# Computing the convolution of the first 1024 tokens with diagonal matmuls instead of a banded matrix and a DRAM bounce

## The chip, the cores and the metric

The kernel runs on one core of one Trainium2 chip. The metric is device time in microseconds (us) of the whole program, the median of several executions. Executions of the same kernel differ by some tenths of a per cent, here by up to 4.8 us (the kernel before, 768.03 to 772.8).

## The reference

The program is a causal convolution with 7 taps over the sequence, followed by a two-layer network with an ELU between the layers. There are 8 heads of 24 channels, and all channels of a head share 7 softmax-normalised taps.

```python
w = softmax(weight, axis=-1)                      # (8 heads, 7 taps)
x_pad = concat([zeros(B, 6, D), x], axis=1)       # x: (8, 4096, 192)
x_unf = x_pad[:, idx, :].reshape(B, S, 7, 8, 24)
att = einsum('hk,bskhg->bshg', w, x_unf).reshape(B * S, 192)
h = att @ w_in                                    # 192 -> 2048
g = where(h > 0, h, exp(minimum(h, 0)) - 1)
out = g @ w_out                                   # 2048 -> 192
```

## The kernel before

The 32,768 tokens are cut into 32 "supers" of 1024 tokens. A super has 16 "pairs" (blocks of 128 of the 2048 hidden columns, for two half supers at once). For each pair TensorE computes H = att @ w_in into one of three PSUM slots, ScalarE computes E = exp(H), GpSimd clips E to at most 1, and VectorE writes gT = max(E - 1, H), which frees the slot. While super s+1 makes its H, TensorE multiplies the gT of super s by w_out ("output matmuls").

The convolution is also done on TensorE: x times a banded matrix `Tm` that holds the 7 taps on its diagonals. The band is built through DRAM: zeros are written, then the taps along the diagonal, and the result is read back into `Tk`. The order of `Tk` is not that of `Tm`, so one engine copies it. The convolved data is evicted to `csb`, bounced through DRAM (`conv_slots`) and gathered into `att`, the layout that the H matmuls need.

```python
# sync engine: the band through DRAM
sy.dma_start(band[...], Tm[...]).then_inc(s_band, 16)             # zeros
W(s_set, 5)                                                       # softmaxed taps are ready
sy.dma_start(diagonal, wprb[...]).then_inc(s_band, 16)            # 128 pieces of 112 bytes
W(s_band, 32)
sy.dma_start(Tk[:], band[:, :, :]).then_inc(s_band, 16)
# ... cut ...
# VectorE, before its loop (super 0 reads Tk itself; Tm is for the later supers)
v.tensor_copy(Tm[:, :, :].rearrange("p h t -> p t h"), Tk[:]).then_inc(s_tm)
# ... cut ...
# ScalarE, each pair n
W(s_h, n + 1)
for u in range(2):
    a.activation(E[:, n % NE, u, :], H[:, k, GS * u : GS * (u + 1)], ACT.Exp).then_inc(s_exp)
```

The convs of the next super are placed at fixed pairs (`EARLY_CONV = {1: (1, 0), 4: (1, 1), 12: (2, 0)}` during super 0).

## Time and profile before

| | before |
|---|---|
| median of the first three runs | 769.51 us (768.03 to 772.8) |
| span of the profiled execution | 767.1 us |
| first H of super 0 starts | 27.41 us |
| first exp starts | 28.27 us |
| first H of super 1 starts | 52.13 us |

The table of busy time by stretches, for 50 to 750 us. The columns are the window and its length, then busy us and instruction count of TensorE, its weight loads, VectorE, ScalarE and GpSimd, then granted clock, DMA share and GB/s.

```profile
50.00:750.00 700.00, 699.84 (x13274) 489.44 (x13270) 610.31 (x992) 620.30 (x1113) 631.59 (x1058) 1.00 0.43 95
```

TensorE is busy for 699.84 of 700 us at full clock. Nothing can be gained there without removing matmuls. What is open is the head.

The head's part of the chain of waits before: start, duration (both us), and what the program was waiting for or doing.

```profile
0.75 2.96 DMA wq<-in_weight_dram
...
5.49 5.64 DMA conv_band<-wprb
...
11.15 4.94 DMA Tk<-conv_band
...
16.13 3.89 PE H L466 x76
...
20.04 1.24 DVE csb L402
...
21.29 2.17 DMA conv_slots<-csb
...
24.88 2.40 DMA att<-conv_slots
...
41.52 9.73 DMA w_out<-in_moe_w_out_dram
```

Seven things follow one another before the first H can start at 27.41: loading the taps, storing the diagonal, reading the band back, the conv, its eviction, the bounce and the gather. The change attacks this chain. Later the chain runs through the w_out load, for which the first output matmul, at 51.30, waited 0.16 us.

### The profile page before, as it was taken

Reading aid. Unit: us, or ns where it says so; the run is one execution under the profiler, and the core shown is the slowest. Engines: PE = TensorE matmul, PEld = TensorE weight load, DVE = VectorE, ACT = ScalarE, POOL = GpSimd, SP = SyncE. Lnnn points to the kernel's source line nnn. Section 1 sums busy time; section 2 is a strip of 40 time slices with the busy share of each in tenths; the row PEclk is TensorE's granted clock in tenths of the full one; section 3 lists DMA queues with packets and bytes.
Section 4 is the critical chain, followed back from the end, with each engine's and each line's share of the span. In section 5 each row is a group of like instructions: output and inputs, shape, how many; then the busy total and the mean of one; then the engine's idle time right before and its main releaser. Section 6 shows DMA issues by size and latency. Waiting matters only on the chain.

```text
span 767.1 us, 32323 instructions
## 1 busy us (share of the span) xinstructions
PE 752.3 (98%) x13910; PEld 515.0 (67%) x13910; DVE 638.7 (83%) x1035; ACT 645.2 (84%) x1155; POOL 661.8 (86%) x1109
## 2 busy tenths in 40 slices
PE   6899999999999999999999999999999999999997
PEld 3347767666766776776776677677676667767766
DVE  1588898898898898889888889888888988988993
ACT  1488888888888988888888888898888898888883
POOL 3498998899898899899889989989989988988892
PEclk8999999999999999999999999999999999999999
DMA  7474344345435435534434543543553443454211
GB/s 119 103 126 107 78 104 96 92 100 114 85 90 113 86 87 114 110 78 101 107 81 100 115 88 87 115 86 89 111 110 78 102 104 83 100 114 91 71 44 63
DMA packets 107919, 73.73 MB, mean 96 GB/s; under 512 B 45408, under 2 KB 106848, under 8 KB 107776
## 3 DMA queue, kind: packets, MB, share of 16 engines
q1 hardware_dynamic: 66344, 55.14, 23.7%
q0 software_dynamic: 40944, 16.13, 19.3%
q8 instruction: 109, 1.79, 1.0%
q10 hardware_dynamic: 488, 0.39, 0.2%
q14 instruction: 34, 0.28, 0.1%
HBM read 44.34 MB, written 42.24 MB: 113 GB/s over the span
## 4 chain that ended last, share of the span: by engine, by line
PE 93%; DMA 4%; DVE 1%; POOL 1%; ACT 0%; issue 0%; SPq 0%; POOLq 0%
PE ops L521 44%; PE H L492 44%; PE H L466 5%; DMA w_out<-in_moe_w_out_dram 1%; DMA conv_band<-wprb 1%; PE H L521 1%; DVE gT L413 1%; DMA Tk<-conv_band 1%; POOL E L310 0%; DMA wq<-in_weight_dram 0%; DMA att<-conv_slots 0%; ACT E L367 0%; DMA conv_slots<-csb 0%; POOL w_in L280 0%; PE ops L445 0%
## 5 line engine op out<-in xcount | busy, mean ns | idle before, releaser
L413 DVE SCALAR_TENSOR_TENSOR gT<-E,H 128x512 f16<-128x512 f32 x1024 | 630.6, 682 | 100.3 <-POOL E L310 92.8
L310 POOL TENSOR_SCALAR E<-E 128x512 f32<-128x512 f32 x1024 | 603.7, 612 | 71.0 <-ACT E L367 67.2
L367 ACT ACTIVATE E<-H 128x512 f32<-128x512 f32 x1024 | 546.1, 605 | 92.8 <-PE H L492 79.2
L521 PEld LDWEIGHTS ops<-w_out,gT 64*128 64x128 f16 x8064 | 342.3, 94 | 109.9 <-ACT osb L341 10.9
L521 PE MATMUL ops<-w_out,gT 64*128 64x192 f16 x8064 | 414.5, 243 | 1.1 <-DVE gT L413 0.9
L492 PE MATMUL H<-att,w_in 64*128 64x512 bf16 x3072 | 407.3, 378 | 3.5 <-DMA att<-conv_slots 2.0
L492 PEld LDWEIGHTS H<-att,w_in 64*128 64x128 bf16 x3072 | 129.8, 94 | 105.5 <-DVE gT L413 5.9
L356 ACT ACTIVATE csb<-H 128x1024 bf16<-128x1024 f32 x63 | 64.5, 1023 | 13.7 <-PE H L466 13.7
L341 ACT ACTIVATE osb<-ops 128x768 f32<-128x768 f32 x63 | 51.6, 818 | 5.1 <-PE ops L521 5.1
L275 POOL DMA_DIRECT2D xg<-in_x_dram x64 | 53.8, 842 | 0.4 <-issue 0.4
L466 PE MATMUL H<-Tm,xg 128*24 128x122 bf16 (+1 forms) x2480 | 40.7, 209 | 0.6 <-DVE gT L413 0.6
L466 PEld LDWEIGHTS H<-Tm,xg 128*24 128x24 bf16 x2480 | 31.3, 92 | 11.2 <-issue 11.2
L445 PE MATMUL ops<-zw 128*128 128x512 bf16 x86 | 24.2, 421 | 1.2 <-DVE zw L378 1.2
L445 PEld LDWEIGHTS ops<-zw 128*128 128x128 bf16 x86 | 7.8, 106 | 15.0 <-issue 8.9
L280 POOL DMA_DIRECT2D w_in<-in_moe_w_in_dram x6 | 3.5, 611 | 15.7 <-DMA att<-conv_slots 15.7
L402 DVE CAST csb<-H 128x1024 bf16<-128x1024 f32 x1 | 1.2, 1225 | 12.4 <-PE H L466 12.4
L466 PE MATMUL H<-Tk,xg 128*24 128x122 bf16 (+1 forms) x80 | 3.9, 363 | 4.7 <-DMA Tk<-conv_band 4.7
L424 DVE COPY osb<-H 128x384 f32<-128x384 f32 x1 | 0.6, 558 | 8.9 <-PE H L521 8.9
L466 PEld LDWEIGHTS H<-Tk,xg 128*24 128x24 bf16 x80 | 2.3, 117 | 6.4 <-DMA Tk<-conv_band 5.2
L521 PE MATMUL H<-w_out,gT 64*128 64x192 f16 x128 | 5.6, 243 | 0.1
L521 PEld LDWEIGHTS H<-w_out,gT 64*128 64x128 f16 x128 | 5.2, 94 | 0.3 <-PE H L521 0.3
L333 ACT ACTIVATE osb<-H 128x384 f32<-128x384 f32 x1 | 0.5, 490 | 4.7 <-PE H L521 4.7
(21 smaller groups left out, 13.3 us busy)
## 6 DMA issues: line engine op xcount, KB each, us to landing
out_dram<-osb SPq DMA_DIRECT2D x127, 192.0 KB, 2.7
conv_slots<-csb SPq DMA_DIRECT2D x64, 256.0 KB, 2.5
att<-conv_slots SPq DMA_DIRECT2D x189, 64.0 KB
xg<-in_x_dram POOLq DMA_DIRECT2D x31, 240.0 KB, 5.1
xg<-in_x_dram POOLq DMA_DIRECT2D x33, 192.0 KB, 4.5
w_in<-in_moe_w_in_dram POOLq DMA_DIRECT2D x6, 128.0 KB, 5.1
w_out<-in_moe_w_out_dram POOLq DMA_DIRECT2D x1, 768.0 KB, 9.7
w_in<-w_in POOLq DMA_DIRECT2D x1, 384.0 KB, 5.1
```

Source lines behind the costliest of these rows:

```text
L275: g.dma_start(xg[:, b, w0:w1, :], src).then_inc(s_x[b][part - 1], 16)
L280: g.dma_start(w_in[0:HP, j, c0:c1], bass.AP(tensor=moe_w_in.tensor, offset=8 * j * FF + c0, ap=[[CPH * FF, HEADS], [FF, 8], [1, c1 - c0]], ...
L310: g.tensor_scalar(out=E[:, n % NE, u, :], in0=E[:, n % NE, u, :], scalar1=1.0, scalar2=0.0, op0=ALU.min, op1=ALU.max,).then_inc(s_clp)
L341: a.activation(osb[:, b, :, :, :].rearrange("p g k d -> p g (k d)"), ops[:, :, 0 : 2 * D], ACT.Copy,).then_inc(s_oev)
L356: a.activation(csb[:, m % 4, :, :], H[:, slot_of_conv[m] % 3, :].rearrange("p (b t) -> p b t", b=2), ACT.Copy,).then_inc(s_ce)
L367: a.activation(E[:, n % NE, u, :], H[:, k, GS * u : GS * (u + 1)], ACT.Exp).then_inc(s_exp)
L402: v.tensor_copy(csb[:, 1, :, :], H[:, slot_of_conv[1] % 3, :].rearrange("p (b t) -> p b t", b=2),).then_inc(s_cd)
L413: v.scalar_tensor_tensor(out=gT[:, s % NG3, q, u, :], in0=E[:, n % NE, u, :], scalar=1.0, in1=H[:, slot_of_pair[n] % 3, GS * u : GS * (u + ...
L445: pe.matmul(ops[:, 0, :], zw[:, 0:P], zw[:], start=True, stop=True)
L466: ins = pe.matmul(H[SLOT * q : SLOT * q + CPH, k % 3, GS * hb + o : GS * hb + o + nc_], xg[:, s % NXB, w, CPH * h : CPH * (h + 1)], Tm[:, ...
L492: ins = pe.matmul(H[:, k % 3, GS * r : GS * (r + 1)], w_in[HP * r : HP * (r + 1), j, FC * q : FC * (q + 1)], att[HP * r : HP * (r + 1), s ...
L521: ins = pe.matmul(acc[:, g, D * kb : D * (kb + 1)], gT[HP * rt : HP * (rt + 1), t % NG3, q, g, t0 : t0 + P], w_out[HP * rt : HP * (rt + 1) ...
```

## The change: its intent and its diff

The first super no longer uses the band or the bounce. x is loaded in plain rows and turned by TensorE with an identity matrix. Then eight matmuls with diagonal weights (`Dg`), accumulated in PSUM, do the 7 taps for two neighbouring tokens. The channel order becomes 3p+j, so w_in can be loaded straight into both halves of the partitions, without an on-chip copy. The band is still built, because the supers from 1 on use it. The diff, cut to what matters here:

```diff
-QA = 8
-WARM = (34, 24, 2)
+WCOLS = ((0, 512), (512, 1280), (1280, 2048))
+WARM = (12, 2)
-EARLY_CONV = {1: (1, 0), 4: (1, 1), 12: (2, 0)}
+EARLY_CONV = {5: (1, 0), 8: (1, 1), 13: (2, 0)}
@@ TensorE, before its loop
+            for i in range(3):
+                for j in range(3):
+                    turn(xt_bank(j)[:, P * i : P * (i + 1)], 3 + 2 * i, j, 0, P)
 ... cut ...
+                for k in range(KSIZE + 1):
+                    for r in range(2):
+                        ins = pe.matmul(head_bank(j, r), Dg[HP*r : HP*(r+1), k : k+2, :],
+                            xT[HP*r : HP*(r+1), j, k : k+GS-1 : 2], start=(k == 0), stop=(k == KSIZE), ...)
@@ VectorE, before its loop
+            W(s_tp, 3)
+            v.tensor_copy(xT[:, 1, PAD : PAD + GS], xt_bank(1)).then_inc(s_xtd)
             W(s_wex, 1)
             v.tensor_reduce(wsum[:], wex[:], AXIS.X, ALU.add).then_inc(s_set)   # taps of the band
 ... cut ...
-            v.tensor_copy(Tm[:, :, :].rearrange("p h t -> p t h"), Tk[:]).then_inc(s_tm)
@@ ScalarE, before its loop (so before its first exp)
+            W(s_hc, 3)
+            a.activation(*head_out(a, 2, 0, 1), ACT.Copy).then_inc(s_ha)
+            W(s_band, 48)
+            a.activation(
+                Tm[:, :, :].rearrange("p h t -> p t h"), Tk[:], ACT.Copy
+            ).then_inc(s_tm)
@@ GpSimd, before its loop
+            load_head(0)      # x of super 0; then an identity by select, load_head(1), load_head(2)
+            load_w_in(0)
+            load_w_in(1)
+            for part in (1, 2):
                 load_x(1, part)
-            W(s_w[0], 48)  ... w_in[HP:P] <- w_in[0:HP], W(s_att[0], ...), load_w_in(1)
+            load_w_in(2)
```

The output rows of super 0 are written in the new token order. Everything from super 1 on is the same work.

More of the change, by code (lines that the diff above doesn't have):

```diff
@@ L30 @@
 LAG = -1
-QA = 8
-WARM = (34, 24, 2)
+WCOLS = ((0, 512), (512, 1280), (1280, 2048))
+Q_PART = (0,) * 4 + (1,) * 6 + (2,) * 6
+WARM = (12, 2)
 HALF_STEPS = (10, 10, 6, 6, 10, 11, 11)
 CONV_AT = ((4, 1, 1), (12, 2, 0))
-EARLY_CONV = {1: (1, 0), 4: (1, 1), 12: (2, 0)}
+EARLY_CONV = {5: (1, 0), 8: (1, 1), 13: (2, 0)}
 XW = 5
@@ L89, in conv_at @@
     def conv_at(s, g):
-        m = 2 * s + g
+        m = 2 * s + g - 2
         slot_of_conv[m] = take_slot(("c", m))
         order.append(("c", m))
-    for g in range(2):
-        conv_at(0, g)
     rounds_at = {}
@@ L141, in sema @@
             return stack.enter_context(nc.semaphore(name))
+        xh = sbuf("xh", [P, 9, D], BF16)
+        ident = sbuf("ident", [P, P], BF16)
+        mask = sbuf("mask", [P, HP], BF16)
+        Dg = sbuf("Dg", [P, 9, HP], BF16)
+        xT = sbuf("xT", [P, 3, GS + 8], BF16)
+        wd = sbuf("wd", [P, KSIZE], FP32)
+        wdm = sbuf("wdm", [P, 1], FP32)
+        wd2 = sbuf("wd2", [P, KSIZE], FP32)
+        wde = sbuf("wde", [P, KSIZE], FP32)
+        wds = sbuf("wds", [P, 1], FP32)
+        wdr = sbuf("wdr", [P, 1], FP32)
         xg = sbuf("xg", [P, NXB, NWIN, D], BF16)
@@ L165, in bass_lightweight_conv__then__act_elu_kernel @@
         s_wq = sema("s_wq")
-        s_w = [sema(f"s_w{i}") for i in range(3)]
+        s_w = [sema(f"s_w{i}") for i in range(4)]
+        s_wd = sema("s_wd")
+        s_xl = [sema(f"s_xl{i}") for i in range(3)]
+        s_id = sema("s_id")
+        s_one = sema("s_one")
+        s_z0 = sema("s_z0")
+        s_v = sema("s_v")
+        s_de = sema("s_de")
+        s_D = sema("s_D")
+        s_tp = sema("s_tp")
+        s_xta = sema("s_xta")
+        s_xtd = sema("s_xtd")
+        s_hc = sema("s_hc")
+        s_ha = sema("s_ha")
+        s_hd = sema("s_hd")
         s_set = sema("s_set")
@@ L169, in bass_lightweight_conv__then__act_elu_kernel @@
         s_scr = sema("s_scr")
-        s_hz = sema("s_hz")
         s_x = [[sema(f"s_x{i}_{g}") for g in range(2)] for i in range(NXB)]
         s_tm = sema("s_tm")
-        s_cd = sema("s_cd")
         s_od = sema("s_od")
-        s_wdp = sema("s_wdp")
         s_z = sema("s_z")
@@ L184, in bass_lightweight_conv__then__act_elu_kernel @@
         s_dw = [sema(f"s_dw{i}") for i in range(4)]
-        s_wd = [sema(f"s_wd{i}") for i in range(2)]
         s_tz = sema("s_tz")
@@ L204, in __call__, with xt_bank, head_bank @@
                     self.eng.wait_ge(sem, value)
-        WCOLS = ((0, P * QA), (P * QA, FF))
         NDMA_ATT = 6
-        x_need, z_need, x_count, z_count = {}, {}, [0] * NXB, 0
-        for s in range(NS):
-            x_count[s % NXB] += 16 + 16 * (s == 0)
-            z_count += s % SPB == 0
-            x_need[s, 0] = x_count[s % NXB]
-            x_need[s, 1] = 16 * (s // NXB + 1)
-            z_need[s] = z_count
+        x_need, z_need = {}, {}
+        for s in range(1, NS):
+            x_need[s, 0] = x_need[s, 1] = 16 * ((s - 1) // NXB + 1)
+            z_need[s] = s // SPB
+        def xt_bank(j):
+            return H[:, j // 2, GS * (j % 2) : GS * (j % 2 + 1)]
+        def head_bank(j, r):
+            if j == 0:
+                return ops[:, r, 0 : GS // 2]
+            return H[:, (0, 2, 0)[j], GS * r : GS * r + GS // 2]
         def conv_read(W, m):
-            if m == 1:
-                W(s_cd, 1)
-            else:
-                W(s_ce, m + (m == 0))
+            W(s_ce, m + 1)
         def out_group(eng, t, half, g):
@@ L225, in out_group @@
             row = SUP * t + GS * g + 2 * P * half
-            eng.dma_start(
-                out[row : row + 2 * P, :].rearrange("(k p) d -> p k d", p=P),
-                osb[:, b, g, :, :],
-            ).then_inc(s_out[b], 16)
+            dst = out[row : row + 2 * P, :].rearrange("(k p) d -> p k d", p=P)
+            if t == 0:
+                dst = bass.AP(
+                    tensor=out.tensor,
+                    offset=(GS * half + 1 - g) * D,
+                    ap=[[2 * D, P], [2 * P * D, 2], [1, D]],
+                )
+            eng.dma_start(dst, osb[:, b, g, :, :]).then_inc(s_out[b], 16)
         def read_att(eng, W, s, g):
-            m = 2 * s + g
+            m = 2 * s + g - 2
             W(s_dw[m % 4], 16 * (m // 4 + 1))
@@ L237, in read_att @@
                     tensor=bounce.tensor,
-                    offset=(2 * P * (s % 2) + 8 * j) * SUP + GS * g,
-                    ap=[[SLOT * SUP, HEADS], [SUP, 8], [1, GS]],
+                    offset=(2 * P * (s % 2) + j) * SUP + GS * g,
+                    ap=[[SLOT * SUP, HEADS], [3 * SUP, 8], [1, GS]],
                 )
@@ L254, in load_x @@
                 if part == 0:
-                    if s:
-                        W(s_x[b][0], x_need[s, 0])
+                    W(s_x[b][0], x_need[s, 0])
                     g.memset(xg[0:PAD, b, 0, :], 0.0).then_inc(s_z)
-                    if s == 0:
-                        g.dma_start(
-                            xg[PAD:P, b, 0, :], x_flat[0 : P - PAD, :]
-                        ).then_inc(s_x[b][0], 16)
                     return
-                if s >= NXB:
-                    W(s_cv, 2 * (s - NXB) + 2)
+                if s > NXB:
+                    W(s_cv, 2 * (s - NXB))
                 if part == 1:
-                    w0, w1, row = int(s == 0), XW, t0 - PAD + CW * (s == 0)
+                    w0, w1, row = 0, XW, t0 - PAD
                 else:
@@ L278, in load_w_in, with load_head @@
                 c0, c1 = WCOLS[k]
-                for j in range(3):
+                for r in range(2):
                     g.dma_start(
-                        w_in[0:HP, j, c0:c1],
-                        bass.AP(
-                            tensor=moe_w_in.tensor,
-                            offset=8 * j * FF + c0,
-                            ap=[[CPH * FF, HEADS], [FF, 8], [1, c1 - c0]],
-                        ),
-                    ).then_inc(s_w[k], 16)
-            for part in range(3):
-                load_x(0, part)
+                        w_in[HP * r : HP * (r + 1), :, c0:c1],
+                        moe_w_in.rearrange("(p j) f -> p j f", j=3)[:, :, c0:c1],
+                    ).then_inc(s_w[k], 16)
+            def load_head(k):
+                slot, tile, count = ((3, 0, 3), (4, 4, 3), (1, 3, 2))[k]
+                g.dma_start(
+                    xh[:, slot : slot + 2 * count - 1 : 2, :] if k < 2 else xh[:, 1:3, :],
+                    bass.AP(
+                        tensor=x_flat.tensor,
+                        offset=tile * P * D,
+                        ap=[[D, P], [(1 if k < 2 else 4) * P * D, count], [1, D]],
+                    ),
+                ).then_inc(s_xl[k], 16)
+            load_head(0)
+            W(s_one, 1)
+            g.affine_select(
+                out=ident[:],
+                in_=ident[:],
+                pattern=[[-1, P]],
+                compare_op=ALU.is_equal,
+                fill=0.0,
+                base=0,
+                channel_multiplier=1,
+            ).then_inc(s_id)
+            load_head(1)
+            load_head(2)
             load_w_in(0)
-            for part in range(3):
+            load_w_in(1)
+            for part in (1, 2):
                 load_x(1, part)
-            W(s_w[0], 48)
-            c0, c1 = WCOLS[0]
-            g.dma_start(w_in[HP:P, :, c0:c1], w_in[0:HP, :, c0:c1]).then_inc(s_wdp, 16)
-            W(s_att[0], 16 * NDMA_ATT)
-            load_w_in(1)
+            load_w_in(2)
             for n in range(NP):
@@ L303, in _gpsimd @@
                         w_out[:, :, :], moe_w_out.rearrange("(q p) d -> p q d", p=FC)
-                    ).then_inc(s_w[2], 16)
+                    ).then_inc(s_w[3], 16)
                 for at, part in X_AT:
@@ L324, in _scalar, with head_out @@
             a.activation(scr[:, 1:2], scr[:, 0:1], ACT.Exp)
+            W(s_v, 3)
+            a.activation(wde[:], wd2[:], ACT.Exp, accum_out=wds[:]).then_inc(s_de)
             W(s_set, 2)
             a.activation(wex[:], wq2[:], ACT.Exp).then_inc(s_wex)
+            W(s_tp, 1)
+            a.activation(
+                xT[:, :, 0:PAD],
+                H[:, 1, GS : GS + 24].rearrange("p (j c) -> p j c", j=3)[:, :, 0:PAD],
+                ACT.Copy,
+            ).then_inc(s_xta)
+            for j in (0, 2):
+                W(s_tp, j + 2)
+                a.activation(xT[:, j, PAD : PAD + GS], xt_bank(j), ACT.Copy).then_inc(s_xta)
+            def head_out(eng, j, r0, r1):
+                src = ops if j == 0 else H[:, (0, 2, 0)[j], :].rearrange("p (r t) -> p r t", r=2)
+                return (
+                    att[:, 0, j, GS // 2 * r0 : GS // 2 * r1].rearrange("p (r t) -> p r t", r=r1 - r0),
+                    src[:, r0:r1, 0 : GS // 2],
+                )
+            W(s_hc, 1)
+            a.activation(*head_out(a, 0, 0, 2), ACT.Copy).then_inc(s_ha)
+            W(s_hc, 3)
+            a.activation(*head_out(a, 2, 0, 1), ACT.Copy).then_inc(s_ha)
+            W(s_band, 48)
+            a.activation(
+                Tm[:, :, :].rearrange("p h t -> p t h"), Tk[:], ACT.Copy
+            ).then_inc(s_tm)
             def evac(t, half):
@@ L349, in _scalar @@
                     m = item[1]
-                    if m == 1:
-                        W(s_dw[0], 16)
-                        read_att(a, W, 0, 0)
-                        continue
                     W(s_cv, m + 1)
@@ L379, in _vector @@
             v.memset(Tm[:], 0.0).then_inc(s_tz)
+            v.memset(ident[:], 1.0).then_inc(s_one)
+            v.memset(xh[:, 0, :], 0.0).then_inc(s_z0)
+            v.memset(Dg[:, ::8, :], 0.0).then_inc(s_z0)
+            W(s_id, 1)
+            v.tensor_tensor(mask[:], ident[:, 0:HP], ident[:, HP:P], ALU.add).then_inc(s_v)
+            W(s_wd, 32)
+            v.tensor_reduce(wdm[:], wd[:], AXIS.X, ALU.max).then_inc(s_v)
+            W(s_v, 2)
+            v.tensor_scalar(
+                out=wd2[:], in0=wd[:], scalar1=wdm[:, 0:1], scalar2=None, op0=ALU.subtract
+            ).then_inc(s_v)
             W(s_wq, 16)
@@ L388, in _vector @@
             ).then_inc(s_set)
+            W(s_de, 1)
+            v.reciprocal(wdr[:], wds[:]).then_inc(s_v)
+            W(s_v, 4)
+            v.scalar_tensor_tensor(
+                out=Dg[:, 1:8, :],
+                in0=mask[:, :].unsqueeze(1).to_broadcast([P, KSIZE, HP]),
+                scalar=wdr[:, 0:1],
+                in1=wde[:, :].unsqueeze(2).to_broadcast([P, KSIZE, HP]),
+                op0=ALU.mult,
+                op1=ALU.mult,
+            ).then_inc(s_D)
+            W(s_tp, 3)
+            v.tensor_copy(xT[:, 1, PAD : PAD + GS], xt_bank(1)).then_inc(s_xtd)
             W(s_wex, 1)
@@ L399, in _vector @@
             ).then_inc(s_set)
-            v.memset(H[:, 0:2, :], 0.0).then_inc(s_hz)
-            W(s_cv, 2)
+            W(s_hc, 2)
             v.tensor_copy(
-                csb[:, 1, :, :],
-                H[:, slot_of_conv[1] % 3, :].rearrange("p (b t) -> p b t", b=2),
-            ).then_inc(s_cd)
-            v.tensor_copy(Tm[:, :, :].rearrange("p h t -> p t h"), Tk[:]).then_inc(s_tm)
+                att[:, 0, 1, :].rearrange("p (r t) -> p r t", r=2),
+                H[:, 2, :].rearrange("p (r t) -> p r t", r=2)[:, :, 0 : GS // 2],
+            ).then_inc(s_hd)
+            W(s_hc, 3)
+            v.tensor_copy(
+                att[:, 0, 2, GS // 2 : GS], H[:, 0, GS : GS + GS // 2]
+            ).then_inc(s_hd)
             for n in range(NP):
@@ L445, in warm, with turn @@
                     pe.matmul(ops[:, 0, :], zw[:, 0:P], zw[:], start=True, stop=True)
-            warm(WARM[0])
+            def turn(dst, slot, j, c0, c1):
+                return pe.matmul(
+                    dst,
+                    xh[:, slot : slot + 2, :].rearrange("p i d -> p (i d)")[:, j::3],
+                    ident[:, c0:c1],
+                    start=True,
+                    stop=True,
+                )
+            warm(WARM[0])
+            W(s_id, 1)
+            W(s_xl[0], 16)
+            W(s_xl[1], 16)
+            for i in range(3):
+                for j in range(3):
+                    turn(xt_bank(j)[:, P * i : P * (i + 1)], 3 + 2 * i, j, 0, P)
+            W(s_xl[2], 16)
+            W(s_z0, 1)
+            for j in range(3):
+                ins = turn(H[:, 1, GS + 8 * j : GS + 8 * j + PAD], 0, j, P - PAD, P)
+            ins.then_inc(s_tp)
+            for j in range(3):
+                turn(xt_bank(j)[:, 3 * P : GS], 1, j, 0, P).then_inc(s_tp)
+            W(s_D, 1)
+            W(s_z0, 2)
+            for j in range(3):
+                W(s_xta, (2, 2, 3)[j])
+                if j:
+                    W(s_xtd, 1)
+                for k in range(KSIZE + 1):
+                    for r in range(2):
+                        ins = pe.matmul(
+                            head_bank(j, r),
+                            Dg[HP * r : HP * (r + 1), k : k + 2, :],
+                            xT[HP * r : HP * (r + 1), j, k : k + GS - 1 : 2],
+                            start=(k == 0),
+                            stop=(k == KSIZE),
+                            tile_position=(HP * r, 0),
+                        )
+                ins.then_inc(s_hc)
             for item in order:
@@ L450, in _tensor @@
                     m = item[1]
-                    s, g = divmod(m, 2)
+                    s, g = divmod(m + 2, 2)
                     if m == 0:
-                        W(s_band, 48)
-                        W(s_hz, 1)
-                    if m == 2:
                         W(s_tm, 1)
@@ L469, in _tensor @@
                                     xg[:, s % NXB, w, CPH * h : CPH * (h + 1)],
-                                    Tm[:, h, PAD + c0 : PAD + c0 + nc_]
-                                    if s
-                                    else Tk[:, PAD + c0 : PAD + c0 + nc_, h],
+                                    Tm[:, h, PAD + c0 : PAD + c0 + nc_],
                                     start=True,
@@ L481, in _tensor @@
                     if n == 0:
+                        W(s_ha, 2)
+                        W(s_hd, 2)
+                    elif n < NQ - 1:
                         warm(WARM[1])
-                    elif n < NQ - 1:
-                        warm(WARM[2])
-                    W(s_w[q // QA], 48)
-                    W(s_wdp if q < QA else s_wd[1], 16)
-                    W(s_att[s % 2], 16 * NDMA_ATT * (s // 2 + 1))
+                    W(s_w[Q_PART[q]], 32)
+                    W(s_att[s % 2], 16 * NDMA_ATT * ((s + 1) // 2))
                     k = slot_of_pair[n]
@@ L502, in _tensor @@
                     _, t, half, r0, r1 = item
-                    W(s_w[2], 16)
+                    W(s_w[3], 16)
                     if (t, half) == last_half:
@@ L536, in _sync @@
             W = Waits(sy)
+            for r in range(2):
+                sy.dma_start(
+                    wd[HP * r : HP * (r + 1), :],
+                    bass.AP(
+                        tensor=weight.tensor, offset=0, ap=[[KSIZE, HEADS], [0, 8], [1, KSIZE]]
+                    ),
+                ).then_inc(s_wd, 16)
             sy.dma_start(
@@ L555, in _sync @@
             sy.dma_start(Tk[:], band[:, :, :]).then_inc(s_band, 16)
-            def copy_w(k):
-                W(s_w[k], 48)
-                c0, c1 = WCOLS[k]
-                sy.dma_start(w_in[HP:P, :, c0:c1], w_in[0:HP, :, c0:c1]).then_inc(s_wd[k], 16)
             for item in order:
@@ L564, in _sync @@
                     m = item[1]
-                    s, g = divmod(m, 2)
+                    s, g = divmod(m + 2, 2)
                     conv_read(W, m)
@@ L570, in _sync @@
                     ).then_inc(s_dw[m % 4], 16)
-                    if m == 1:
-                        read_att(sy, W, 0, 1)
-                        copy_w(1)
-                    elif m == 2 or g == 1:
+                    if m == 0 or g == 1:
                         read_att(sy, W, s, g)
```

## The prediction

> **What bounds it now.** TensorE. The table by stretches gives it 699.8 busy us out of 700 between 50 and 750 us, granted clock 1.00; the change touches nothing there (the 3p+j order only re-addresses equal-sized transfers). Only the head is open: the first exp starts at 28.3 us and the output matmuls start at 51.3 us (timeline).
>
> **The head before.** The chain of waits is serial: weight load 3.0 us, softmax 1.7, band diagonal store 5.6, band read-back 4.9, conv matmuls 3.9, eviction 1.2, bounce write 2.2, gather 2.4-4, so H begins at 27.4. From there, 15 pairs take about 23 us, paced by GpSimd and VectorE (1.3 us per pair, plus about 1 us per conv taking a PSUM slot).
>
> **What the change does to the first super.** x lands at about 7.5-8.5 us (the old loads took 3.5-7.1 us), turns under 1 us, one 128x512 copy about 0.6, 48 taps of 256 columns, about 2.6 us warm or 5.2 cold (the trace has a 512-column pair at 0.22 warm), half-bank copies 0.7. So H would start at about 13-15 us: about 13 us earlier.
>
> **Why most of that will not be cashed.** ScalarE's program now waits for the read-back band and copies it into Tm *before its first exp*. VectorE computes the band weights only *after* its copy of xT. So the band chain starts later than before: wprb at about 9.9 us instead of 5.4; diagonal store about 5.6 (it was 5.6 for 14 KB, with the DMA engines saturated); read-back about 5; hence Tk at about 20.5-21. W_in is now fetched twice, so the DMA load is no lighter. [...] the 14 KB store took 5.6 us under load, an earlier 28 KB load 3.0. Then the Tm copy, 1.2-2.6 us (VectorE took 2.58 for it). First exp at about 22-23.5 us: 5-6 us earlier, not 13.
>
> **The first 15 pairs after.** Again about 23 us; the convs move to pairs 5, 8 and 13, about 0.5 us better since none disturbs the fill. Against it, TensorE fills three slots by about 16 us and idles about 8 us, so it resumes at half clock ([...]before, the granted clock was 0.50 from 14 to 20 us after an idle from 11.4). With two warming matmuls per pair that costs about 1 us. Output matmuls start at about 46.5 us instead of 51.3; after that nothing changes.
>
> **Sum.** 28.3 to 22.9 is -5.4, the cold clock +1.0, the better conv order -0.5: about -5 us. Predicted 764.5 us, 8 in 10 between 760.0 and 768.0. Chances: faster by over 2% 0.02, within 2% 0.975, slower 0.005. Even 13 us would be under 2%.
>
> **Right or wrong in the profile.**
> - First H before 16 us, but first exp after 21, with ScalarE's Tm copy directly before it, waiting for the DMA Tk.
> - Diagonal store issued at about 10 us; the head's chain runs through wprb, store, read-back, Tm, exp.
> - Granted clock 0.5 around 20-26 us.
> - Output matmuls from about 46.5; afterwards supers of 22.65 us as before.
>
> **What would make it wrong.** Store and read-back at 2-3 us each would give 5 us more. A slow select on GpSimd delays x and all after it; a slow Tm copy, or w_in or w_out landing late, would eat the gain.

## The result, and the profile after

The changed kernel took 771.22 us in the median of 4 runs (770.73 to 771.55), beside 769.61 us for the kernel before. The ratio is 1.0018 with a 95% interval of 0.9995 to 1.0042: the same within the noise. A ratio is the mean time of one kernel's fast runs over that of the other's of the same rounds, so it is not quite the ratio of the medians. The prediction of 764.5 (760 to 768) was wrong: there was no gain at all.

| time stamps of the profiled execution, us | before | after | difference |
|---|---|---|---|
| first H of super 0 | 27.41 | 15.33 | -12.1 |
| first exp | 28.27 | 25.38 | -2.9 |
| H of pair 6 | 37.55 | 35.48 | -2.1 |
| H of pair 10 | 42.72 | 43.15 | +0.4 |
| first output matmul | 51.30 | 51.90 | +0.6 |
| first H of super 1 | 52.13 | 54.01 | +1.9 |
| span | 767.1 | 768.9 | +1.8 |

The first H came 12.1 us earlier, as hoped, and by the end of the first super all of it was gone. The rest of the program adds nothing: from the first H of super 1 to the end takes 767.1 - 52.13 = 714.97 us before and 768.9 - 54.01 = 714.89 us after. In all 14 kernels that rest lies between 714.6 and 715.0 us. So one time stamp, the first H of super 1, decides the span, and it is the number to follow below.

The head's part of the chain of waits after, in the same form as before:

```profile
2.56 6.01 DMA xh<-in_x_dram
...
8.70 0.87 PE H L530 x14
...
11.17 5.49 DMA conv_band<-wprb
...
16.67 4.20 DMA Tk<-conv_band
...
20.89 4.97 ACT Tm L384
...
28.37 1.46 PE H L608 x6
...
41.70 6.94 DMA conv_slots<-csb
...
49.90 4.06 DMA att<-conv_slots
...
54.01 0.82 PE H L608 x6
```

Of the new conv only the turn with the identity matrix (L530) is on this chain. From there it runs through the band: the store, the read-back, and then a copy of Tm on ScalarE that takes 4.97 us and stands before the first exp. Later a second stretch appears, where the chain before had the w_out load: the bounce of super 1's second half takes 6.94 us, and its gather 4.06.

The timeline after shows the matmuls of H around the gap: start, duration, engine, line, what, and in brackets the idle time before it and what ended it.

```profile
15.33 0.82 PE L608 MATMUL H<-att,w_in 64*128 64x512 bf16 x6 [0.56 <-ACT att L382]
...
17.92 0.82 PE L608 MATMUL H<-att,w_in 64*128 64x512 bf16 x6
...
20.89 4.97 ACT L384 ACTIVATE Tm<-Tk 128x1088 bf16<-128x1088 bf16 x1 [5.71 <-DMA Tk<-conv_band]
...
28.37 1.46 PE L608 MATMUL H<-att,w_in 64*128 64x512 bf16 x6 [9.09 <-DVE gT L495]
...
30.73 1.46 PE L608 MATMUL H<-att,w_in 64*128 64x512 bf16 x6
...
54.01 0.82 PE L608 MATMUL H<-att,w_in 64*128 64x512 bf16 x6 [1.12 <-DMA att<-conv_slots]
```

Three pairs fill the three PSUM slots by 18.7 us. Then TensorE idles 9.09 us, because no exp has run. When it resumes, a pair takes 1.46 us instead of 0.82 and pairs come 2.36 us apart instead of 1.3. At 54.01 it waits for a DMA.

The busy table of the kernel after shows why those pairs are slow; the third number from the right is the granted clock, and the last is GB/s.

```profile
15.00:20.00 5.00, 3.94 (x24) 1.02 (x24) 0.23 (x1) 0.19 (x1) 0.00 (x0) 1.00 1.00 192
20.00:25.00 5.00, 0.00 (x0) 0.00 (x0) 0.00 (x0) 4.11 (x1) 0.00 (x0) 0.89 0.00 2
25.00:30.00 5.00, 1.63 (x7) 0.42 (x8) 2.97 (x5) 3.84 (x8) 3.49 (x6) 0.50 0.00 0
30.00:35.00 5.00, 5.00 (x57) 1.28 (x56) 3.27 (x6) 2.57 (x6) 3.26 (x5) 0.58 0.00 0
```

Between 20 and 25 us TensorE did nothing and ScalarE was in its copy; from 24.0 to 34.2 us the clock was at half (read from windows of 0.5 us). The DMA engines, which moved 192 GB/s until 20 us, were then empty. The same windows show an earlier stretch at half clock, from 10.3 to 13.7 us, in which most of the new conv ran: it took from 10.28 to 14.77 us here, and from 9.53 to 12.48 in c5 below, whose granted clock stayed at 1.00.

### The profile page after: what moved, and what is told of

The parts are those of the page before. It is cut to its first block, busy times and chain, and to the rows that moved or that the text cites. A ratio compares the mean times of both kernels' runs of the same rounds, so it can differ in the third digit from the quotient of the medians.

```text
span 768.9 us, 32206 instructions
## 1 busy us (share of the span) xinstructions
PE 746.5 (97%) x13847; PEld 512.7 (67%) x13847; DVE 636.8 (83%) x1043; ACT 651.1 (85%) x1162; POOL 661.7 (86%) x1108
## 4 chain that ended last, share of the span: by engine, by line
PE 93%; DMA 4%; ACT 1%; DVE 1%; SPq 0%; issue 0%; POOL 0%; POOLq 0%
PE ops L637 44%; PE H L608 44%; PE H L584 5%; DMA conv_slots<-csb 1%; DMA xh<-in_x_dram 1%; PE H L637 1%; DMA conv_band<-wprb 1%; ACT Tm L384 1%; DMA Tk<-conv_band 1%; DMA att<-conv_slots 1%; DVE gT L495 0%; SPq L265 0%; ACT E L423 0%; PE ops L527 0%; POOL E L343 0%
## 5 line engine op out<-in xcount | busy, mean ns | idle before, releaser
L608 PE MATMUL H<-att,w_in 64*128 64x512 bf16 x3072 | 409.2, 379 | 13.7 <-DVE gT L495 12.0
L412 ACT ACTIVATE csb<-H 128x1024 bf16<-128x1024 f32 x62 | 63.5, 1024 | 0.0
L293 POOL DMA_DIRECT2D xg<-in_x_dram x62 | 52.2, 841 | 0.4 <-issue 0.4
L527 PE MATMUL ops<-zw 128*128 128x512 bf16 x40 | 14.6, 482 | 1.2 <-DVE zw L434 1.2
L384 ACT ACTIVATE Tm<-Tk 128x1088 bf16<-128x1088 bf16 x1 | 5.0, 4969 | 5.7 <-DMA Tk<-conv_band 5.7
L527 PEld LDWEIGHTS ops<-zw 128*128 128x128 bf16 x40 | 3.2, 112 | 9.8 <-issue 8.3
L305 POOL DMA_DIRECT2D xh<-in_x_dram x3 | 2.4, 818 | 0.8 <-POOLq L719 0.8
```

The lines of the kernel that those rows point to most:

```text
L293: g.dma_start(xg[:, b, w0:w1, :], src).then_inc(s_x[b][part - 1], 16)
L384: a.activation(Tm[:, :, :].rearrange("p h t -> p t h"), Tk[:], ACT.Copy).then_inc(s_tm)
L412: a.activation(csb[:, m % 4, :, :], H[:, slot_of_conv[m] % 3, :].rearrange("p (b t) -> p b t", b=2), ACT.Copy,).then_inc(s_ce)
L527: pe.matmul(ops[:, 0, :], zw[:, 0:P], zw[:], start=True, stop=True)
L608: ins = pe.matmul(H[:, k % 3, GS * r : GS * (r + 1)], w_in[HP * r : HP * (r + 1), j, FC * q : FC * (q + 1)], att[HP * r : HP * (r + 1), s ...
```

## The experiments

Theory A: the first exp waits for ScalarE's Tm copy, that copy waits for the band, and the first super's end follows the first exp; what was left of the gain then went to the half clock and to late data for super 1. Theory B: the end of the first super is set by the arrival of super 1's data, so an earlier first exp changes nothing. All runs gave correct results.

| run | what it does to the kernel after | first H of super 1 | median us | ratio to before (95%) |
|---|---|---|---|---|
| (after) | | 54.01 | 771.22 | 1.0018 (0.9995 to 1.0042) |
| e1_band_early | begins the band chain 5 us earlier | 54.77 | 768.90 | 0.9994 (0.9969 to 1.0019) |
| e2_tm_dve | Tm copy on VectorE, after pair 2 | 45.68 | 762.52 | 0.9917 (0.9896 to 0.9938) |
| e3_keep_warm | 40 warming matmuls in the gap | 52.28 | 769.19 | 1.0007 (0.9984 to 1.0030) |
| e4_w_out_early | w_out load at pair 1 | 51.96 | 768.25 | 0.9990 (0.9970 to 1.0010) |
| e5_band_quiet | e1, and other loads wait for the band | 46.02 | 763.53 | 0.9928 (0.9913 to 0.9943) |
| e6_tm_order | ScalarE's copy walked the other way | 51.93 | 767.93 | 0.9986 (0.9971 to 1.0001) |
| e7_conv_early | super 1's convs at pairs 3 and 6 | 51.91 | 768.55 | 0.9995 (0.9978 to 1.0011) |
| c1_dve_wout | e2 and e4 | 44.81 | 761.86 | 0.9907 (0.9891 to 0.9924) |
| c2_band_first | e5, w_out at pair 1, early copy on VectorE | 44.59 | 761.35 | 0.9901 (0.9886 to 0.9916) |
| c3_direct | c1 without any Tm copy | 44.44 | 761.09 | 0.9889 (0.9871 to 0.9906) |
| c4_dve_order | c1, VectorE's copy walked the other way | 42.10 | 758.69 | 0.9872 (0.9858 to 0.9886) |
| c5_direct_early | c3 with e1's early band chain | 39.19 | 756.94 | 0.9844 (0.9829 to 0.9858) |

### e2: the Tm copy taken off ScalarE

```diff
-            W(s_band, 48)                                     # ScalarE, before its loop
-            a.activation(Tm[...].rearrange("p h t -> p t h"), Tk[:], ACT.Copy).then_inc(s_tm)
+                if n == 3:                                    # VectorE, in its loop
+                    W(s_band, 48)
+                    v.tensor_copy(Tm[...].rearrange("p h t -> p t h"), Tk[:]).then_inc(s_tm)
```

> Only the Tm copy is moved: off ScalarE, to VectorE after its third pair. Theory A: first exp at about 16.2 us; the copy takes about 2.6 us on VectorE as in the kernel before; [...]first H of super 1 at about 45 us (25.4 to 16.2 is -9, the copy's stall +2.6, the cold clock -3), the whole about 762 us. Theory B: first exp at 16.2, but first H of super 1 not before 52, time about 770.

The first exp started at 16.85 us and the first H of super 1 at 45.68, which is 8.3 us earlier than after. Theory A said about 45, theory B not before 52, so B falls. The timeline of e2:

```profile
21.96 2.58 DVE L489 COPY Tm<-Tk 128x1088 bf16<-128x1088 bf16 x1
...
25.88 0.65 PE L585 MATMUL H<-Tm,xg 128*24 128x122 bf16 x40 [2.61 <-DVE gT L496]
```

The copy took 2.58 us on VectorE, and the gap that it left on TensorE was 2.61 us. The clock did not fall: it was granted in full from 15 us on. But the copy still stalls the pairs, and super 1's data was still late (the first H of super 1 waited 0.83 us for `att`).

### e1 and e5: why the band is late

In the kernel after, VectorE computes the band's taps only after its copy of xT, so the diagonal store is issued at 11.17 us instead of 5.49. The prediction made this the reason for the late band. e1 moves the taps forward again:

```diff
-            W(s_v, 3)                                          # ScalarE: exp for Dg first
-            a.activation(wde[...]) ; W(s_set, 2) ; a.activation(wex[...])
+            W(s_set, 2) ; a.activation(wex[...]) ; W(s_v, 3) ; a.activation(wde[...])
@@ VectorE: the whole softmax of the band's taps (wmx .. wprb) before the wait for s_wd and s_tp
@@ sync engine: wq is loaded first; the two wd loads go behind the zero store
```

> Only the band chain is moved forward: the weights are loaded first and the band weights are computed before the xT copy. Theory A (the first exp waits for ScalarE's Tm copy, that copy for the band, and the first super's end follows the first exp): the diagonal store is issued at about 5.5 us instead of 11.2, Tk lands at about 16 instead of 20.9, the Tm copy still takes about 5.0 us, the first exp starts at about 20.5 instead of 25.4, the first H of super 1 at about 49 instead of 54.0, the whole is about 5 us shorter (about 766). Theory B (the end of the first super is set by the arrival of super 1's data, whose bounce runs beside the w_out load): the first exp is 5 us earlier all the same, but the first H of super 1 stays at about 53 to 54 and the time within 1 us of the change's.

Both theories missed, because they shared a wrong assumption. The first exp did not move. The chain of waits of e1:

```profile
6.12 8.45 DMA conv_band<-wprb
14.58 6.74 DMA Tk<-conv_band
21.35 4.97 ACT Tm L384
```

The store was issued 5 us earlier (6.12 against 11.17), but store and read-back took 8.45 + 6.74 = 15.2 us instead of 5.49 + 4.20 = 9.7, and Tk landed at 21.3 us instead of 20.9. The median was 768.9, with runs from 767.66 to 771.47; the trace is that of the slowest run. The spans of the other three, 765.9 to 767.6 us, less the rest of about 714.9 us put their first H of super 1 at about 51.0 to 52.7 us (an estimate), 1 to 3 us before the 54.01 of the kernel after. No trace of those runs was kept, so that beginning earlier gained nothing is shown for one run only. e5 begins equally early and also keeps the other loads back:

```diff
             load_w_in(0)
+            W(s_band, 48)
             load_w_in(1)
```

> As e1 (band chain first), and the loads after the first w_in part wait until the band has been read back; ScalarE's Tm copy stays before the first exp. In e1 the store and the read-back took 8.5 and 6.7 us, so Tk landed at 21.3 us although it was begun 5 us earlier. If that is traffic of the weight and x loads: store and read-back together take under 8 us instead of 15.2, Tk lands at about 13 to 14, the Tm copy runs at about 15 to 20 (ScalarE has the head's copies first), the first exp starts at about 20.5 and, by theory A, the first H of super 1 at about 48 to 50, time about 765. If the two DMAs are slow in themselves (tiny or strided pieces): they still take over 12 us and the first exp stays at 25 or later.

The DMA view of e5 (queue, count, size, us to landing) and its timeline:

```profile
Tk<-conv_band SPq DMA_DIRECT2D x1, 272.0 KB, 2.7
...
conv_band<-wprb SPq DMA_DIRECT2D x1, 14.0 KB, 5.3
```

```profile
10.75 0.32 SPq L679 DMA_DIRECT2D Tk<-conv_band  x1
...
15.27 5.00 ACT L385 ACTIVATE Tm<-Tk 128x1088 bf16<-128x1088 bf16 x1
...
19.77 3.36 ACT L424 ACTIVATE E<-H 128x512 f32<-128x512 f32 x6
```

Store and read-back took 5.3 + 2.7 = 8.0 us, so Tk was there 10.75 + 2.7 = 13.4 us after the start. The same two transfers, begun within 0.7 us of the same moment, took 15.2 us in e1 beside the loads of w_in and x. The traffic made the difference of 7.2 us. What the pieces cost in themselves is not separated: with the later loads held back, the 14 KB store still took 5.3 us, while the 272 KB store of zeros in the same run took 2.6. e5 also repeats the test of theory A: the first exp went from 25.38 to 19.77 (-5.6) and the first H of super 1 from 54.01 to 46.02 (-8.0). The second gain is larger because TensorE's gap was 3.31 us instead of 9.09 and the pairs after it came 1.3 us apart: the slow pairs did not come.

### e6: why the copy took 4.97 us

The prediction had allowed 1.2 to 2.6 us for it. e6 walks the same copy in the other order:

```diff
-                Tm[:, :, :].rearrange("p h t -> p t h"), Tk[:], ACT.Copy
+                Tm[:], Tk[:, :, :].rearrange("p t h -> p h t"), ACT.Copy
```

> Only the order in which ScalarE's Tm copy walks is changed: contiguous writes with strided reads instead of contiguous reads with strided writes. If the strided write is what makes it 4.97 us (a 128x1024 copy takes 1.02 us on the same engine): it takes about 1.1 to 1.3 us, the first exp starts at about 21.7 instead of 25.4, time about 3 us shorter. If the strided side costs the same whichever it is: about 5 us again and the same time.

```profile
21.32 2.12 ACT L384 ACTIVATE Tm<-Tk 128x1088 bf16<-128x1088 bf16 x1 [5.53 <-DMA Tk<-conv_band]
```

The copy fell from 4.97 to 2.12 us. Writing single bf16 elements 272 bytes apart had cost 4.97/1088 = 4.6 ns an element; writing in order and reading 16 bytes apart costs 1.9 ns. So the order of the walk was most of it, though not all: the expectation of 1.1 to 1.3 us was missed. Two things changed at once, the side that is strided (writes or reads) and the stride (272 or 16 bytes), and no run separates them. The first exp moved to 23.34 us (-2.0) and the first H of super 1 to 51.93 (-2.1).

### e3: the half clock

```diff
-                        warm(WARM[1])
+                        warm(40 if n == 3 else WARM[1])
```

> Only the number of warming matmuls before pair 3 is changed (2 to 40), so that TensorE is busy through the wait of 9 us. If the cold clock is a cost of its own: granted clock 1.00 from 19 us on, pairs 3 to 5 are 1.3 us apart instead of 2.36, pair 6 starts at about 33 us instead of 35.5, and the time falls by 2 to 3 us. If what ends the first super is the arrival of super 1's data: pair 6 is earlier, but the time falls by less than 1 us.

Busy table of e3, to be compared with the same windows of the kernel after:

```profile
20.00:25.00 5.00, 5.00 (x25) 2.27 (x24) 0.00 (x0) 3.90 (x1) 0.00 (x0) 1.00 0.01 3
25.00:30.00 5.00, 3.33 (x19) 1.09 (x19) 2.72 (x5) 4.49 (x9) 3.36 (x6) 1.00 0.00 0
```

The clock stayed at 1.00. Pairs 3, 4 and 5 were 1.3 us apart, pair 6 started at 33.45 instead of 35.48, and the first H of super 1 came 1.7 us earlier. So the half clock cost about 2 us, of which 1.7 reached the end. The median, 769.19, agrees, though against the kernel before it is not separable from 1.

### e4 and e7: super 1's late data

The bounce of super 1's second half is issued at 41.7 us in the kernel after, in the middle of the w_out load, whose 768 KB are issued at 39.8 and take 9.4 us. e4 moves the load away, and e7 moves the convs away:

```diff
-W_OUT_AT = 8                                          # e4
+W_OUT_AT = 1
-EARLY_CONV = {5: (1, 0), 8: (1, 1), 13: (2, 0)}      # e7
+EARLY_CONV = {3: (1, 0), 6: (1, 1), 13: (2, 0)}
```

> Only the place of the w_out load is changed (at pair 1 instead of pair 8). If the bounce write of super 1's second half is slow (6.9 us) because it shares the DMA engines with w_out: it lands in about 2.4 us, the first H of super 1 no longer waits for a DMA (1.1 us now) and starts at about 52 to 53 instead of 54.0; time 1 to 2 us shorter. If the bounce is slow for another reason: it still takes over 5 us and the first H of super 1 still waits for it.

> Only the places of super 1's two convs are changed: at pairs 3 and 6 instead of 5 and 8; w_out stays at pair 8. If the late arrival of super 1's data is a collision of its second bounce with the w_out load: the bounce is issued at about 37 us, before w_out at about 40, lands in under 5 us instead of 6.9, the first H of super 1 waits for no DMA and starts at 52 to 53 instead of 54.0, time 1 to 2 us under the change's (771.2). If the early slots cost the pairs more than the wait did: first H of super 1 at 54 or later and the same time.

In e4 the bounces issued between 36 and 45 us landed in 2.2 to 2.5 us; in e7 the slowest bounce took 4.0. In both the wait for `att` is gone, and the first H of super 1 came at 51.96 and 51.91 us, 2.1 us earlier. To see where the 2.1 us were won, take the timelines from the w_out load and the second bounce to the last pair of super 0 and the first H of super 1. The kernel after (its first H of super 1, at 54.01, is shown above):

```profile
39.83 1.20 POOL L335 DMA_DIRECT2D w_out<-in_moe_w_out_dram  x1
...
41.70 0.45 SPq L685 DMA_DIRECT2D conv_slots<-csb  x1
...
51.24 0.82 PE L608 MATMUL H<-att,w_in 64*128 64x512 bf16 x6 [1.15 <-DVE gT L495]
```

e4, and then e7:

```profile
50.48 0.82 PE L608 MATMUL H<-att,w_in 64*128 64x512 bf16 x6 [1.14 <-DVE gT L495]
...
51.96 0.81 PE L608 MATMUL H<-att,w_in 64*128 64x512 bf16 x6
```

```profile
50.43 0.82 PE L608 MATMUL H<-att,w_in 64*128 64x512 bf16 x6 [1.15 <-DVE gT L495]
...
51.91 0.81 PE L608 MATMUL H<-att,w_in 64*128 64x512 bf16 x6
```

From the last pair to the first H of super 1 it takes 2.77 us in the kernel after and 1.48 in e4 and in e7. Two different edits that separate the same two transfers both remove these 1.3 us, so the collision is the cause of that part. The other 0.8 us were won before the last pair, and the collision does not explain them. In e4, GpSimd no longer spends 1.20 us at 39.83 on issuing w_out, and pair 10 no longer waits 1.12 us for a slot; in e7 the convs disturb other pairs. No run splits this part further.

The kernel before had the same two transfers side by side:

```profile
41.52 1.22 POOL L302 DMA_DIRECT2D w_out<-in_moe_w_out_dram  x1
...
42.05 0.45 SPq L567 DMA_DIRECT2D conv_slots<-csb  x1
```

There the bounce was issued 0.53 us after w_out and landed in 3.2 us; in the kernel after it was issued 1.87 us after w_out and took 6.94. No run puts the convs back at pairs 1, 4 and 12, so how much of this the new places brought is not shown.

### c1 to c5: versions meant to be faster

> e2 and e4 together (Tm copy on VectorE after pair 2, w_out load at pair 1). If the two costs are separate, the gains add: first H of super 1 at about 43 to 44 us (e2 45.7), no DMA wait there, time about 760.5 to 761. If w_out was only late because all was late: as e2.

c1 (e2 and e4 together) gained only 0.9 us over e2, not the 2: its first H of super 1 is at 44.81. VectorE's copy now took 2.88 us, TensorE idled 2.96 us, and the clock then fell once more (a pair at 27.72 us took 1.46 us instead of 0.82).

> A version meant to be faster: e5's quiet band, w_out load at pair 1, and the Tm copy on VectorE before its head copies, where VectorE is idle. Theory A: Tk lands at about 13, the copy's 2.6 us delay the first H by at most 2 us (16 to 17), no copy in the loop, first H of super 1 at about 41 to 43, time about 759. If the early loads then come too late (w_in for pair 4, x for super 1): waits for DMA in the first pairs, and no gain over e2.

c2 reached 44.59 us. The band was early (store 5.4, read-back 2.7 us), but GpSimd then had its six remaining loads to issue from 13.79 to 19.76 us, and its first clip came only at 19.8. The first H came at 17.02 us, later than e2's 15.99, and the granted clock was 0.75 from 15 to 20 us (a pair at 18.96 us took 1.46 us). This was neither of the outcomes. The late clip of GpSimd, which issues the loads, is one cost that the trace shows; no run separates it from the other two.

c3 removes the Tm copy: the band lies in DRAM in the order of Tm, and the read-back goes straight into it.

```diff
-    band = nc.dram_tensor("conv_band", (P, TW, HEADS), BF16).ap()
+    band = nc.dram_tensor("conv_band", (P, HEADS, TW), BF16).ap()
-                ap=[[HEADS * (TW + 1), P], [1, KSIZE * HEADS]],
+                ap=[[HEADS * TW + 1, P], [TW, HEADS], [1, KSIZE]],
-            sy.dma_start(Tk[:], band[:, :, :]).then_inc(s_band, 16)
+            sy.dma_start(Tm[:], band[:, :, :]).then_inc(s_tm, 16)
```

> A version meant to be faster: c1 without any Tm copy. The band lies in DRAM in the order of Tm, so that the read-back goes straight into Tm; the diagonal store then has 1024 pieces of 14 bytes instead of 128 of 112. Theory A (what gates the first exps and stalls the loop is the copy): no copy in the loop, [...]first H of super 1 at about 40 to 41 us instead of c1's 44.8, time about 757.5 to 758.5. If the store of many small pieces takes over 10 us: the band lands after 24 us, the first conv of super 1 waits for it, and the gain over c1 is under 1 us.

```profile
11.33 9.11 DMA conv_band<-wprb
20.45 5.68 DMA Tm<-conv_band
...
26.17 1.04 PE H L580 x38
```

The 1024 small pieces took 9.11 us to store, where the 128 pieces of c1 took 5.3, and super 1's first conv waited for the band until 26.17 us. That is the second outcome of the expectation: hardly any gain over c1 (44.44 against 44.81). The six runs of c3 fall in two groups, four at 760.9 to 761.4 us and two at 758.4 and 758.6; the trace is of the slower group, and why the two were faster is open.

> c1, with VectorE's Tm copy walked with contiguous writes and strided reads, as in e6 on ScalarE (4.97 to 2.12 us). If the strided write costs the same on VectorE: the copy falls from 2.9 to about 1.3 us, first H of super 1 about 1.5 us earlier, time about 760. If VectorE's 2.6 us are not from the write order: as c1.

With the order of e6, VectorE's copy took 1.45 us instead of 2.88, and the first H of super 1 came at 42.10, 2.7 us before c1. That is more than the copy itself saved; c4 shows no slow pair after the copy as c1 does (the pair after it took 0.82 us in c4 and 1.46 in c1; granted clock from 25 to 30 us: 1.00 in c4, 0.72 in c1), so the clock accounts for some of the rest; how much was not tested.

> c3 with the band chain begun first, as in e1. e1 showed that beginning earlier under the same traffic lands at the same time (about 21 us). If that holds here, the time is that of c3 within noise; if the many small pieces make c3's band late, this recovers it.

c5 is c3 with the band chain begun at 5.28 us. Its store took 10.3 us and the read-back 5.9, so Tm landed at about 21.5 us, when the first conv of super 1 needed it:

```profile
13.04 0.82 PE L604 MATMUL H<-att,w_in 64*128 64x512 bf16 x6 [0.57 <-ACT att L382]
...
13.90 1.08 ACT L419 ACTIVATE E<-H 128x512 f32<-128x512 f32 x2 [1.00 <-PE H L604]
...
21.54 0.65 PE L580 MATMUL H<-Tm,xg 128*24 128x122 bf16 x40 [0.33 <-DMA Tm<-conv_band]
```

The first exp follows the first H at once, the conv waits 0.33 us, and the granted clock was 1.00 from the turn of x at 7.93 us to the last matmul. (The trace is of the fastest of the four runs; the mean clock of the other three was 0.998.) So the early start recovered what c3 had lost, the second outcome of the expectation: begun 6.05 us earlier than in c3, the band landed 4.6 us earlier, unlike in the trace of e1. The first H of super 1 is at 39.19 us, 12.9 us earlier than in the kernel before. The median is 756.94 us beside 768.37, ratio 0.9844 (1.6% shorter): the gain that the change was made for.

## Why the prediction was wrong, point by point

- **Right: what bounds the kernel and where the change acts.** The steady part took the same time to 0.1 us, and the first H came at 15.33 us (predicted about 13 to 15, and before 16).
- **Right: most of the gain is not cashed, and the Tm copy before the first exp, with its wait for the band, is why.** e2 moved that copy alone and got 8.3 us.
- **Wrong in size: "Then the Tm copy, 1.2-2.6 us (VectorE took 2.58 for it). First exp at about 22-23.5 us".** The copy took 4.97 us and the first exp started at 25.4. A duration from one engine was carried to another engine, though the access was strided; e6 shows that the order of the walk alone makes it 2.12 or 4.97 us on ScalarE. On the same engine a 128x1024 eviction took 1.02 us. Against the 22.9 us used in the sum, the first exp was 2.5 us late.
- **Wrong in size: "that costs about 1 us" (the half clock).** e3 shows 2.0 us at pair 6, 1.7 at the end of the super. The clock was at half from 24.0 to 34.2 us, not "around 20-26 us", because the gap came later: TensorE's last matmul before it ended at 19.3 us.
- **Failed: "The first 15 pairs after. Again about 23 us; the convs move to pairs 5, 8 and 13, about 0.5 us better" and "after that nothing changes".** From the first exp to the first output matmul took 26.5 us (25.38 to 51.90; before 23.0), so the output matmuls began at 51.90 us and not at 46.5. From there to the first H of super 1 took 2.1 us instead of 0.8, because its data was late. e7 shows that the places of the convs cost 2.1 us against places at pairs 3 and 6; against the old places they were not tested, so that the term has the wrong sign is likely and not shown. The prediction named w_out landing late as a risk, but not that w_out would delay something else.
- **Right number, half the reason: the late band.** Tk landed at 20.9 us (predicted 20.5 to 21), with the store issued late and the two transfers about as long as predicted (5.49 and 4.20 us; 5.6 and 5). But the late taps are not enough of a reason: in the trace of e1 they came 5 us earlier and the band landed at 21.3. It landed early (13.4 and 13.5 us) only in e5 and c2, where the other loads were also held back.
- **The sum.** The prediction put the output matmuls, and all after them, about 4.9 us earlier. By the time stamps, the first exp came 2.5 us later than its 22.9, the stretch to the first output matmul took about 2.9 us more than its 23.6 (46.5 - 22.9), and the first H of super 1 came 1.3 us later still. -4.9 + 2.5 + 2.9 + 1.3 = +1.8, beside +1.9 measured (the median moved by +1.6). Of the 2.9 us, about 1.0 is the half clock (2.0 instead of 1.0) and up to 0.8 is what e4 and e7 win before the last pair; about 1.1 is left open.

## What to carry to other kernels

When a stage is made ready earlier, look at what each consuming engine has in its program before it: here one set-up copy on ScalarE, with its wait for the band, held back 9 us of a 12 us gain. What runs beside a transfer nearly doubled its time here (store and read-back 15.2 us in e1, 8.0 in e5), so starting it earlier into the same traffic may gain little (in e1 the store began 5 us earlier and Tk landed at 21.3 us instead of 20.9), and moving it can put it under another one (the bounce took 6.94 us beside the w_out load, and 2.2 to 2.5 in e4). Do not carry the duration of a strided copy from one engine to another (2.58 us on VectorE in e2, 4.97 on ScalarE in the kernel after); in c5 the cheapest copy was the one that a different layout in DRAM made unnecessary.

## What the runs measured of copies, transfers and the clock

- A copy of 128x1088 bf16 elements on ScalarE took 4.97 us with writes 272 bytes apart (the kernel after) and 2.12 us with reads 16 bytes apart (e6), while a 128x1024 eviction from PSUM took 1.02 us there.
- The copy with strided writes (272 bytes) took 2.3 times as long as the one with strided reads (16 bytes) on ScalarE (4.97 and 2.12 us) and 2.0 times on VectorE (2.88 us in c1 and 1.45 in c4). Side and stride are not separated.
- The 14 KB diagonal store took 5.3 us in e5 and 8.4 us in e1, and the 272 KB read-back 2.7 and 6.7 us.
- The clock was at half for 3.4 us (after, 10.3 to 13.7), 6.8 us (before, 13.5 to 20.3) and 10.2 us (after, 24.0 to 34.2). Before these falls TensorE had idled since 9.61 us, after 0.91 us of work and an idle of 2.15 us before that (after, at 10.3), since 11.38 us (before, at 13.5) and since 19.3 us (after, at 24.0); the clock was back 3.4, 4.2 and 5.8 us after TensorE resumed, at 10.28, 16.13 and 28.37 us. An idle of 2.61 us in e2 left the clock at 1.00 (20 to 30 us), and after one of 3.31 us in e5 the pairs took 0.82 us, as at full clock. So the length of one idle alone does not tell in these traces whether the clock falls, and no run tests what does. (Before the first change the view shows 1.00, although the warming matmuls of the kernel before start 0.42 us apart until 6.7 us and 0.21 us after it; so the start of a trace is not counted here.)
